# Grouped attention over a cache: K, P and q transposed as 32-bit words of two bf16, scores in 64-row tiles

## The chip, the cores and the metric

The kernel runs on one core of one Trainium2 chip. The metric is device time in microseconds from start to end of one execution; the figure compared is the median of several runs. It is written engine by engine: TensorE (PE), VectorE (DVE), ScalarE (ACT), GpSimd (POOL) and the sync engine (SP), which issues nearly all DMAs. Each engine works through its own list in order, and semaphores tie the lists together.

## What is computed

```python
B, Sq, D = 32, 4, 1024
Hq, Hkv, Sk, Dh = 32, 4, 2048, 128          # everything bf16
q = (x @ wq).reshape(B, Sq, Hq, Dh).transpose(0, 2, 1, 3)
k = jnp.repeat(k_cache, Hq // Hkv, axis=1)  # k_cache, v_cache: [B, Hkv, Sk, Dh]
v = jnp.repeat(v_cache, Hq // Hkv, axis=1)
scores = jnp.einsum("bhqd,bhkd->bhqk", q, k) * (Dh ** -0.5)
p = softmax(scores)
o = jnp.einsum("bhqk,bhkd->bhqd", p, v)
return o.transpose(0, 2, 1, 3).reshape(B, Sq, Hq * Dh) @ wo
```

A batch has 32 query rows for each of the four K/V heads (8 query heads times 4 tokens): the 128 rows of its score matrix are 4 heads times 32. K and V are 2 MB each per batch, and 32 batches of both are 134 MB of the 151 MB that are read.

## The kernel before

**Loads.** SP issues x, four slices of wq (each holds two of the eight slices `kt` of the contraction), K of batches 0 to 2, and then, batch by batch, K of batch b + 3 and V of batch b. There are three buffers each: K of batch b waits until the last K fill of batch b - 3 is done (line 149), V of batch b until the PV product of batch b - 3 is (line 158). Four slices of wo go between, over the memory of wq. The last V comes in four pieces, one for each head (line 161).

**q.** x is transposed (line 185) and q is projected with weight slices as the stationary operand (line 192): 8 slices times 32 heads, 128 x 128 each, so that q comes out with the head dimension on the partitions. Eight copies on DVE and ACT (lines 203 and 205) bring it to `QT_sb`.

**One batch.** K arrives with sequence rows on the partitions and has to be turned so that the head dimension is on them. `pe_fill` (line 223) does that with 64 bf16 transposes of 128 x 128, eight to a PSUM bank, in `NFILL` = 8 fills; `evac` copies each fill to `KT_sb`, fills 2, 3, 5 and 7 on DVE (line 233) and the others on ACT (line 235). The banks come from a ring of four (`slot`), and whoever takes a bank waits for the copy that empties it. `pe_qk` makes the scores: four column tiles of 32 (one per head) times four chunks of 512 sequence positions; the weights of a tile are loaded with the first chunk (line 260), and the other three use them again (`_matmul_held`, line 16). Then follow the maximum on DVE (line 300), exp on ACT with a running sum (line 305), 16 bf16 transposes of P (`pe_pt`, line 241) with two copies on DVE (line 247), 64 matmuls of P with V (`pe_pv`, line 268), the division by the sum on ACT (line 285), and one transpose of the result (line 291). Every eight batches the output projection runs (line 316).

**The order.** PE's list for step i: scores of batch i, the transpose of result i - 3, the fills of batch i + 1, PV of batch i - 2, the transposes of P of batch i. On ACT exp of batch i stands between the copies of fills 1 and 4, on DVE the maximum stands ahead of all copies of the step. Ahead of step 0 come x, q and the fills of batch 0. After the last step come PV of batch 30, the last PV head by head (line 380), and the last output projection with it.

Of the kernel before, what the change touches and what calls it, by code (L numbers as in the profile page):

```python
# [5 lines left out]
ACT = mybir.ActivationFunctionType  # L6
# [6 lines left out]
def _matmul_held(nc, eng, out, lhsT, rhs, tile_position, start, stop):  # L13


    return eng.add_instruction(mybir.InstMatmult(  # L16
        name=nc.get_next_instruction_name(),
        engine=eng.engine,
        start_tensor_calc=start,
        stop_tensor_calc=stop,  # L20
        tile_size=(128, 32),
        tile_position=tile_position,
        ldweights=False,
        ins=[eng.lower_ap(rhs), eng.lower_ap(lhsT, for_matmul_weights=True)],
        outs=[eng.lower_ap(out)],
    ))
# [46 lines left out]
def bass_standalone__gqa_block_cached__sampling_kernel(  # L73
# [12 lines left out]
    NT = B * Sq  # L86
# [5 lines left out]
    TV = T // C  # L92
    KT = D // 128
    NKB = 3
    NVB = 3
    NFILL = 8
    TB = T // NFILL
# [10 lines left out]
    with ExitStack() as es:  # L108
# [7 lines left out]
        KT_sb = sbuf("KT_sb", [128, TV, G, R * C], BF16)  # L116
        QT_sb = sbuf("QT_sb", [128, B, Hq, Sq], BF16)
        oT_sb = sbuf("oT_sb", [128, Hq, NT], BF16)
        P_sb = sbuf("P_sb", [128, Sk], BF16)
        PT_sb = sbuf("PT_sb", [128, 2, TV, 128], BF16)  # L120
# [3 lines left out]
        y_sb = sbuf("y_sb", [128, NOG, NC], BF16)  # L124
        ident = sbuf("ident", [128, 128], BF16)
        mx = sbuf("mx", [128, B], F32)
        negmx = sbuf("negmx", [128, B], F32)
        ssum = sbuf("ssum", [128, B], F32)
        rinv = sbuf("rinv", [128, B], F32)
# [5 lines left out]
        def ps_q(h):  # L135
            t = ps_s if h < 16 else ps_r[:, :, :].rearrange("p a b -> p (a b)")
            return t[:, (h % 16) * 128:(h % 16 + 1) * 128]
# [32 lines left out]
        for b in range(B):  # L170
# [10 lines left out]
            pattern=[[-1, 128]], channel_multiplier=1), ["ident0"], "ident")  # L181

# [6 lines left out]
        p.op("dve", lambda e: e.tensor_copy(xT_sb.rearrange("p a b -> p (a b)"), ring[2].bitcast(BF16)), ["xT"], "xT_evac")  # L189
        for kt in range(KT):  # L190
            for h in range(Hq):
                p.op("pe", lambda e, kt=kt, h=h: e.matmul(  # L192
                    ps_q(h), lhsT=w_sb[:, kt, h * Dh:(h + 1) * Dh], rhs=xT_sb[:, kt, :],
                    start=(kt == 0 and h % 4 == 0), stop=(kt == KT - 1), skip_group_check=True),
                    ["xT_evac", ("wq", kt // 2)],
                    ("qproj" if h == Hq - 1 else ("q", h // 4)) if kt == KT - 1 and h % 4 == 3 else None)
        for j in (4, 5, 6, 7, 0, 1, 2, 3):
            src = (ps_s if j < 4 else ps_r[:, :, :].rearrange("p a b -> p (a b)"))[:, (j % 4) * 512:(j % 4 + 1) * 512]
            src = src.rearrange("p (hh b s) -> p hh b s", hh=4, b=B, s=Sq)
            dst = QT_sb[:, :, 4 * j:4 * j + 4, :].rearrange("p b hh s -> p hh b s")  # L200
            w = "qproj" if j == Hq // 4 - 1 else ("q", j)
            if j % 2 == 0:
                p.op("dve", lambda e, s=src, d=dst: e.tensor_copy(d, s), [w], ("qe", j))  # L203
            else:
                p.op("act", lambda e, s=src, d=dst: e.activation(d, s, ACT.Copy), [w], ("qe", j))  # L205


        freed = [("qe", 4 + n) for n in range(NRING)]
# [8 lines left out]
        def pe_fill(b, f):  # L217
            buf, waits = slot(("kt", b, f))
            buf = slot_of["kt", b, f] = buf.bitcast(BF16)
            for q in range(TB):  # L220
                c, v = q // (TB // C), q % (TB // C)
                t = c * TV + f * TB // C + v
                p.op("pe", lambda e, q=q, t=t: e.transpose(  # L223
                    buf[:, q * 128:(q + 1) * 128], K_sb[:, b % NKB, t, :], ident[:, :]),
                    waits + [("k", b), "ident"] if q == 0 else [], ("fill", b, f) if q == TB - 1 else None)

        def evac(b, f):
            buf = slot_of["kt", b, f]
            waits = [("fill", b, f)] + ([("qk", b - 1)] if b else [])
            dst = KT_sb[:, f * TB // C:(f + 1) * TB // C, :, :].rearrange("p v g (r c) -> p (v g) r c", c=C)  # L230
            src = buf.rearrange("p (c m r) -> p m r c", c=C, r=R)
            if f in DVE_FILLS:
                p.op("dve", lambda e: e.tensor_copy(dst, src), waits, ("kt", b, f))  # L233
            else:
                p.op("act", lambda e: e.activation(dst, src, ACT.Copy), waits, ("kt", b, f))  # L235

        def pe_pt(i, f, ready):
            buf, waits = slot(("pt", i, f))
            buf = slot_of["pt", i, f] = buf.bitcast(BF16)
            for q in range(8):  # L240
                p.op("pe", lambda e, q=q: e.transpose(  # L241
                    buf[:, q * 128:(q + 1) * 128], P_sb[:, (8 * f + q) * 128:(8 * f + q + 1) * 128], ident[:, :]),
                    waits + [ready] if q == 0 else [], ("ptf", i, f) if q == 7 else None)

        def evac_pt(i, f):
            buf = slot_of["pt", i, f]
            p.op("dve", lambda e: e.tensor_copy(PT_sb[:, i % 2, 8 * f:8 * f + 8, :].rearrange("p t q -> p (t q)"), buf),  # L247
                 [("ptf", i, f)] + ([("pv", i - 2)] if i > 1 else []), ("pt", i, f))


        def pe_qk(i):
            waits = [("kt", i, f) for f in range(NFILL)]
            waits += [("qe", j) for j in range(Hq // 4)] if i == 0 else [("exp", i - 1)]
            for c in range(4):
                for g in range(G):
                    out = ps_s[32 * g:32 * (g + 1), c * 512:(c + 1) * 512]
                    lhsT = QT_sb[:, i, REP * g:REP * (g + 1), :]
                    rhs = KT_sb[:, 4 * c:4 * (c + 1), g, :]
                    if c == 0:
                        mm = lambda e, a=(out, lhsT, rhs), g=g: e.matmul(  # L260
                            a[0], lhsT=a[1], rhs=a[2], start=True, stop=True, tile_position=(0, 32 * g))
                    else:
                        mm = lambda e, a=(out, lhsT, rhs), g=g: _matmul_held(
                            nc, e, *a, tile_position=(0, 32 * g), start=True, stop=True)
                    p.op("pe", mm, waits, ("qk", i) if (c, g) == (3, G - 1) else None)

        def pv_mm(buf, i, g, t, waits, done):
            p.op("pe", lambda e: e.matmul(  # L268
                buf[32 * g:32 * (g + 1), 0:Dh],
                lhsT=PT_sb[:, i % 2, t, 32 * g:32 * (g + 1)],  # L270
                rhs=V_sb[:, i % NVB, g, t, :],
                start=(t == 0), stop=(t == TV - 1), tile_position=(0, 32 * g)), waits, done)
# [10 lines left out]
        def o_evac(i):  # L283
            buf = slot_of["o", i]
            p.op("act", lambda e: e.activation(o_sb[:, :], buf[:, 0:Dh], ACT.Copy, scale=rinv[:, i:i + 1]),  # L285
                 [("pv", i), ("rinv", i)] + ([("oT", i - 1)] if i else []), ("o", i))
# [6 lines left out]
        def ot_evac(i):  # L293
            buf = slot_of["ot", i]
            p.op("act", lambda e: e.activation(  # L295
                oT_sb[:, :, i * Sq:(i + 1) * Sq], buf[:, 0:128].rearrange("p (h s) -> p h s", s=Sq), ACT.Copy),
                [("oT", i)], ("ot", i))

        def softmax_max(i):
            p.op("dve", lambda e: e.tensor_reduce(mx[:, i:i + 1], ps_s[:, :], AX.X, ALU.max), [("qk", i)], ("mx", i))  # L300
            p.op("dve", lambda e: e.tensor_scalar(negmx[:, i:i + 1], mx[:, i:i + 1], -scale, None, op0=ALU.mult),  # L301
                 [("mx", i)], ("negmx", i))

        def softmax_exp(i):
            p.op("act", lambda e: e.activation(  # L305
                P_sb[:, :], ps_s[:, :], ACT.Exp, bias=negmx[:, i:i + 1], scale=scale, accum_out=ssum[:, i:i + 1]),
                [("negmx", i)] + ([("ptf", i - 1, 1)] if i else ["qproj"]), ("exp", i))

        def softmax_rinv(i):
            p.op("dve", lambda e: e.reciprocal(rinv[:, i:i + 1], ssum[:, i:i + 1]), [("exp", i)], ("rinv", i))  # L310


        def oproj_mm(buf, n, heads, waits, done):
            for h in heads:
                for j in range(4):
                    p.op("pe", lambda e, h=h, j=j: e.matmul(  # L316
                        buf[32 * j:32 * (j + 1), 0:NC],
                        lhsT=oT_sb[:, h, 32 * n:32 * (n + 1)],
# [22 lines left out]
        for i in range(B):  # L341
# [20 lines left out]
            if i == L:  # L362
                p.op("dve", lambda e: e.tensor_scalar(P_sb[:, :], P_sb[:, :], rinv[:, L:L + 1], None, op0=ALU.mult),  # L363
# [13 lines left out]
        def pv_last(g):  # L377
            buf, waits = slot(None)
            for t in range(TV):
                p.op("pe", lambda e, t=t: e.matmul(  # L380
                    buf[:, 0:32], lhsT=V_sb[:, L % NVB, g, t, :], rhs=PT_sb[:, L % 2, t, 32 * g:32 * (g + 1)],
# [4 lines left out]
                oT_sb[:, 8 * g:8 * (g + 1), L * Sq:(L + 1) * Sq], buf[:, 0:32].rearrange("p (h s) -> p h s", s=Sq)),  # L386
# [73 lines left out]
```

## Time and profile before

| | |
|---|---|
| median of 6 runs | 383.03 us (382.2 to 384.02) |
| profiled execution | 382.05 us |
| its span | 380.3 us |
| PE, DVE, ACT busy | 277.0, 274.8, 207.4 us (73%, 72%, 55%) |
| PE weight loads busy | 217.6 us (57%) |
| PE instructions | 5927 matmuls and transposes, 5543 weight loads |
| moved by DMA | 152.3 MB, 401 GB/s over the span |

The profile is of one execution. Busy time of an engine is the time in which at least one of its instructions ran; durations in a group are means of one instruction, and PE's overlap each other, so that the distance between two is shorter than the duration of one. The chain that ended last is followed back from the last instruction, at each step to what released it. "L223" is line 223 of the kernel. q1 is the queue of the program's own transfers, q8 that of its instructions.

### The profile page before, as it was taken

To read this page: it belongs to the slowest core of one execution; us is meant where nothing else is said; L and a number is where in the kernel's file an instruction comes from. 1 tells how busy PE (TensorE), PEld (TensorE's weight loads), DVE (VectorE), ACT (ScalarE), POOL (GpSimd) and SP (SyncE) were. 2 spreads that over 40 slices of the span, in tenths; PEclk is the share of its full clock that TensorE was granted. 3 is DMA by queue.
4 is the path that set the end of the run, shared out by engine and by line. 5 is a ranking of instruction groups with operands and counts; after the bars stand their busy time and mean duration, and the time that the engine had idled before them with its cause. 6 is when DMAs were issued, how large, how long until landed. Compare 5 with 4: busy or idle time off the path is not lost.

```text
span 380.3 us, 12207 instructions
## 1 busy us (share of the span) xinstructions
PE 277.0 (73%) x5927; PEld 217.6 (57%) x5543; DVE 274.8 (72%) x302; ACT 207.4 (55%) x259; POOL 0.7 (0%) x6
## 2 busy tenths in 40 slices
PE   2876878883837677788777777878777678877756
PEld 1874656662726555566555556656555456655545
DVE  0006999995538395699988884989888776998741
ACT  1005777771615461677666664677666446766630
POOL 0000000000000000000000000000000000000000
PEclk9998999999768699999999999999999999999989
DMA  8999999999999999999999999999999999999981
GB/s 331 427 429 431 413 410 418 411 394 410 402 411 410 423 414 417 411 416 415 418 415 418 415 417 418 415 419 416 416 415 415 415 416 424 415 417 408 370 320 44
DMA packets 27250, 152.30 MB, mean 401 GB/s; under 512 B 1472, under 2 KB 1984, under 8 KB 22592
## 3 DMA queue, kind: packets, MB, share of 16 engines
q1 hardware_dynamic: 27104, 151.49, 97.5%
q8 instruction: 45, 0.74, 0.8%
q10 hardware_dynamic: 96, 0.03, 0.0%
q14 instruction: 5, 0.04, 0.0%
HBM read 151.26 MB, written 0.26 MB: 398 GB/s over the span
## 4 chain that ended last, share of the span: by engine, by line
DMA 56%; PE 17%; ACT 13%; DVE 10%; issue 2%; SPq 1%
DMA K_sb<-in_k_cache_dram 56%; ACT KT_sb L235 7%; ACT P_sb L305 6%; DVE KT_sb L233 5%; PE ps_r L223 4%; DVE mx L300 4%; PE ps_r L316 3%; PE ps_r L268 3%; PE ps_r L241 3%; PE ps_s L16 2%; PE ps_s L316 1%; PE ps_s L260 1%; DVE PT_sb L247 1%; PE ps_r L380 0%; SPq L145 0%
## 5 line engine op out<-in xcount | busy, mean ns | idle before, releaser
L223 PE MATMUL ps_r<-ident,K_sb 128*128 128x128 bf16 x2048 | 139.9, 226 | 59.3 <-DMA K_sb<-in_k_cache_dram 34.8
L233 DVE COPY KT_sb<-ps_r 128x1024 bf16<-128x1024 bf16 x128 | 147.9, 1217 | 31.1 <-PE ps_r L223 30.9
L223 PEld LDWEIGHTS ps_r<-ident,K_sb 128*128 128x128 bf16 x2048 | 122.3, 101 | 78.2 <-DMA K_sb<-in_k_cache_dram 35.6
L235 ACT ACTIVATE KT_sb<-ps_r 128x1024 bf16<-128x1024 bf16 x128 | 124.3, 1026 | 70.3 <-PE ps_r L223 70.3
L300 DVE TENSOR_REDUCE mx<-ps_s 128x1 f32<-128x2048 f32 x32 | 73.3, 2292 | 6.1 <-PE ps_s L16 2.1
L305 ACT ACTIVATE P_sb<-ps_s,negmx 128x2048 bf16<-128x2048 f32 x32 | 63.1, 1970 | 2.1 <-DVE negmx L301 2.1
L247 DVE COPY PT_sb<-ps_r 128x1024 bf16<-128x1024 bf16 x64 | 41.3, 686 | 18.6 <-PE ps_r L241 17.0
L268 PE MATMUL ps_r<-V_sb,PT_sb 128*32 128x128 bf16 x1984 | 34.2, 222 | 18.4 <-ACT KT_sb L235 13.5
L268 PEld LDWEIGHTS ps_r<-V_sb,PT_sb 128*32 128x32 bf16 x1984 | 28.7, 98 | 23.7 <-ACT KT_sb L235 21.3
L295 ACT ACTIVATE oT_sb<-ps_r 128x128 bf16<-128x128 bf16 x31 | 8.6, 278 | 54.1 <-PE ps_r L291 54.1
L241 PE MATMUL ps_r<-ident,P_sb 128*128 128x128 bf16 x512 | 35.0, 223 | 3.0 <-DVE P_sb L363 2.5
L241 PEld LDWEIGHTS ps_r<-ident,P_sb 128*128 128x128 bf16 x512 | 29.4, 99 | 6.6 <-DVE P_sb L363 2.7
L16 PE MATMUL ps_s<-KT_sb,QT_sb 128*32 128x512 bf16 x384 | 27.0, 387 | 0.0
L291 PEld LDWEIGHTS ps_r<-ident,o_sb 128*128 128x128 bf16 x31 | 3.0, 98 | 26.1 <-issue 26.1
L203 DVE CAST QT_sb<-ps_r 128x512 bf16<-128x512 f32 x2 | 1.3, 686 | 22.4 <-PE ps_r L192 22.4
L285 ACT ACTIVATE o_sb<-ps_r,rinv 128x128 bf16<-128x128 f32 x31 | 11.4, 367 | 11.1 <-PE ps_r L268 11.1
L316 PE MATMUL ps_r<-w_sb,oT_sb 128*32 128x256 bf16 x384 | 11.8, 273 | 5.3 <-issue 4.1
L205 ACT ACTIVATE QT_sb<-ps_r 128x512 bf16<-128x512 f32 x2 | 1.1, 594 | 25.9 <-PE ps_r L192 25.9
L260 PE MATMUL ps_s<-KT_sb,QT_sb 128*32 128x512 bf16 x128 | 13.0, 396 | 2.5 <-DVE KT_sb L233 1.7
L192 PE MATMUL ps_s<-P_sb,w_sb 128*128 128x128 bf16 x128 | 9.3, 231 | 7.5 <-DMA w_sb<-in_wq_dram 7.5
L316 PEld LDWEIGHTS ps_r<-w_sb,oT_sb 128*32 128x32 bf16 x384 | 10.1, 97 | 6.5 <-issue 5.4
L192 PEld LDWEIGHTS ps_s<-P_sb,w_sb 128*128 128x128 bf16 x128 | 8.1, 104 | 8.0 <-issue 4.3
(27 smaller groups left out, 65.8 us busy)
## 6 DMA issues: line engine op xcount, KB each, us to landing
K_sb<-in_k_cache_dram SPq DMA_DIRECT2D x32, 2048.0 KB, 25.2
V_sb<-in_v_cache_dram SPq DMA_DIRECT2D x31, 2048.0 KB, 27.0
w_sb<-in_wq_dram SPq DMA_DIRECT2D x4, 2048.0 KB, 14.6
w_sb<-in_wo_dram SPq DMA_DIRECT2D x4, 2048.0 KB, 24.1
V_sb<-in_v_cache_dram SPq DMA_DIRECT2D x4, 512.0 KB, 11.4
P_sb<-in_x_dram SPq DMA_DIRECT2D x1, 256.0 KB, 2.7
out_dram<-y_sb SPq DMA_DIRECT2D x14, 16.0 KB, 9.4
out_dram<-y_sb ACTq DMA_DIRECT2D x2, 16.0 KB, 1.8
```

Of the source, the lines that this page charges most:

```text
L16: return eng.add_instruction(mybir.InstMatmult(name=nc.get_next_instruction_name(), engine=eng.engine, start_tensor_calc=start, stop_tenso ...
L192: p.op("pe", lambda e, kt=kt, h=h: e.matmul(ps_q(h), lhsT=w_sb[:, kt, h * Dh:(h + 1) * Dh], rhs=xT_sb[:, kt, :], start=(kt == 0 and h % 4 ...
L223: p.op("pe", lambda e, q=q, t=t: e.transpose(buf[:, q * 128:(q + 1) * 128], K_sb[:, b % NKB, t, :], ident[:, :]), waits + [("k", b), "iden ...
L233: p.op("dve", lambda e: e.tensor_copy(dst, src), waits, ("kt", b, f))
L235: p.op("act", lambda e: e.activation(dst, src, ACT.Copy), waits, ("kt", b, f))
L241: p.op("pe", lambda e, q=q: e.transpose(buf[:, q * 128:(q + 1) * 128], P_sb[:, (8 * f + q) * 128:(8 * f + q + 1) * 128], ident[:, :]), wai ...
L247: p.op("dve", lambda e: e.tensor_copy(PT_sb[:, i % 2, 8 * f:8 * f + 8, :].rearrange("p t q -> p (t q)"), buf), [("ptf", i, f)] + ([("pv", ...
L260: mm = lambda e, a=(out, lhsT, rhs), g=g: e.matmul(a[0], lhsT=a[1], rhs=a[2], start=True, stop=True, tile_position=(0, 32 * g))
L268: p.op("pe", lambda e: e.matmul(buf[32 * g:32 * (g + 1), 0:Dh], lhsT=PT_sb[:, i % 2, t, 32 * g:32 * (g + 1)], rhs=V_sb[:, i % NVB, g, t, : ...
L300: p.op("dve", lambda e: e.tensor_reduce(mx[:, i:i + 1], ps_s[:, :], AX.X, ALU.max), [("qk", i)], ("mx", i))
L305: p.op("act", lambda e: e.activation(P_sb[:, :], ps_s[:, :], ACT.Exp, bias=negmx[:, i:i + 1], scale=scale, accum_out=ssum[:, i:i + 1]), [( ...
L316: p.op("pe", lambda e, h=h, j=j: e.matmul(buf[32 * j:32 * (j + 1), 0:NC], lhsT=oT_sb[:, h, 32 * n:32 * (n + 1)], rhs=wo_sb[:, h, NC * j:NC ...
```

## The change

Two neighbouring bf16 values are taken as one 32-bit word and transposed as such, with a float identity. A 128 x 128 transpose of words moves two sequence rows of K (or two columns of P, or two halves of heads of q) at once. What comes out has, on partition r, word r of each row pair.

- K: a fill is four transposes of words in place of eight of bf16. Word r < 64 of a pair of rows holds elements 2r and 2r + 1 of the first row's head dimension, word r >= 64 those of the second row. So `KT_sb` has even and odd elements interleaved, the first rows of the pairs on partitions 0 to 63 and the second rows on 64 to 127. Each transpose writes every fourth word of a bank, and the copy is of 512 contiguous words.
- Scores: 64-row tiles. The lower half of the partitions makes the scores of the even rows, the upper half those of the odd rows, into different banks. The even and the odd elements of the head dimension (`w`) are two matmuls that add up. That is 32 matmuls of 512 columns in place of 16, and 16 weight loads in place of 4: `half` 0 loads the weights, `half` 1 uses them again. `TT` is 8, `DW` 64.
- Exp reads the two halves of the banks in turn, so that P comes out in the order of the sequence. P is transposed in 8 words' transposes instead of 16, its copies are of 512 words, and PV reads its weights in steps of two elements.
- q: x is now the stationary operand and wq the moving one (64 matmuls of 512 columns, weights loaded once per `kt`), which puts tokens on the partitions; eight copies bring q to `q_sb` (in the memory of `KT_sb`), 33 transposes of words turn it, and nine copies bring it to `QT_sb` (33 head slots, since the upper half needs each head shifted by one).
- To make room, the output and half of the transposed result lie over parts of `QT_sb` that are used up, and the per-batch statistics have four columns.

```diff
-def _matmul_held(nc, eng, out, lhsT, rhs, tile_position, start, stop):
+def _matmul_held(nc, eng, out, lhsT, rhs, tile_size, tile_position, start, stop):
...
-    NFILL = 8
-    TB = T // NFILL
+    NFILL = TT
...
-        KT_sb = sbuf("KT_sb", [128, TV, G, R * C], BF16)
-        QT_sb = sbuf("QT_sb", [128, B, Hq, Sq], BF16)
+        KT_sb = sbuf("KT_sb", [128, TT, G, R * C, 2], BF16)
+        q_sb = KT_sb[:, :, :, :, :].rearrange("p a g n w -> p (a g n w)")[:, 0:(Hq + 2) * Dh]
+        QT_sb = sbuf("QT_sb", [128, B, Hq + 1, Sq, 2], BF16)
...
+        p.op("pool", lambda e: e.tensor_copy(identf[:], ident[:]), ["ident"], "identf")
+        for h in (0, Hq + 1):
+            p.op("pool", lambda e, h=h: e.memset(q_sb[:, h, :], 0.0), [], ("qpad", h))
...
         for kt in range(KT):
-            for h in range(Hq):
-                p.op("pe", lambda e, kt=kt, h=h: e.matmul(
-                    ps_q(h), lhsT=w_sb[:, kt, h * Dh:(h + 1) * Dh], rhs=xT_sb[:, kt, :],
...
+            for j in QJ:
+                out, lhsT, rhs = ps_q(j), xT_sb[:, kt, :], w_sb[:, kt, 512 * j:512 * (j + 1)]
+...
+        NQ = (Hq + 1 + 3) // 4
+        for m in range(NQ):
+            slots = range(4 * m, min(4 * m + 4, Hq + 1))
+            buf = ps_q(m % 4)
+            for n, c in enumerate(slots):
...
+                waits += ([("qe", m - 4)] if m >= 4 else [("qs", m)]) if n == 0 else []
+                p.op("pe", lambda e, n=n, c=c, buf=buf: e.transpose(
+                    buf[:, 128 * n:128 * (n + 1)], words(q_sb[:, c:c + 2, :].rearrange("p h d -> p (h d)")), identf[:, :]),
+                    waits, ("qt", m) if c == slots[-1] else None)
+...
         def pe_fill(b, f):
-            for q in range(TB):
...
-                p.op("pe", lambda e, q=q, t=t: e.transpose(
-                    buf[:, q * 128:(q + 1) * 128], K_sb[:, b % NKB, t, :], ident[:, :]),
+            for c in range(C):
+                t = 2 * (c * TT + f)
+                p.op("pe", lambda e, c=c, t=t: e.transpose(
+                    buf.rearrange("p (n c) -> p n c", c=C)[:, :, c],
+                    words(K_sb[:, b % NKB, t:t + 2, :].rearrange("p t d -> p (t d)")), identf[:, :]),
...
         def evac(b, f):
-            dst = KT_sb[:, f * TB // C:(f + 1) * TB // C, :, :].rearrange("p v g (r c) -> p (v g) r c", c=C)
-            src = buf.rearrange("p (c m r) -> p m r c", c=C, r=R)
+            dst = words(KT_sb[:, f, :, :, :].rearrange("p g n w -> p (g n w)"))
...
         def pe_pt(i, f, ready):
-            for q in range(8):
+            for q in range(4):
                 p.op("pe", lambda e, q=q: e.transpose(
-                    buf[:, q * 128:(q + 1) * 128], P_sb[:, (8 * f + q) * 128:(8 * f + q + 1) * 128], ident[:, :]),
+                    buf[:, q * 128:(q + 1) * 128], words(P_sb[:, (4 * f + q) * 256:(4 * f + q + 1) * 256]), identf[:, :]),
...
         def pe_qk(i):
-            for c in range(4):
-                for g in range(G):
-                    out = ps_s[32 * g:32 * (g + 1), c * 512:(c + 1) * 512]
-                    lhsT = QT_sb[:, i, REP * g:REP * (g + 1), :]
-                    rhs = KT_sb[:, 4 * c:4 * (c + 1), g, :]
...
+            for w in range(2):
+                for half in range(2):
+                    for g in range(G):
+                        for par in range(2):
+                            rows = slice(DW * par, DW * (par + 1))
+                            out = ps_s[32 * g:32 * (g + 1), (2 * par + half) * 512:(2 * par + half + 1) * 512]
+                            lhsT = QT_sb[rows, i, REP * g + 1 - par:REP * (g + 1) + 1 - par, :, w]
+                            rhs = KT_sb[rows, 4 * half:4 * half + 4, g, :, w]
+...
         def softmax_exp(i):
             p.op("act", lambda e: e.activation(
-                P_sb[:, :], ps_s[:, :], ACT.Exp, bias=negmx[:, i:i + 1], scale=scale, accum_out=ssum[:, i:i + 1]),
+                P_sb[:, :].rearrange("p (n a) -> p n a", a=2), ps_s[:, :].rearrange("p (a n) -> p n a", a=2), ACT.Exp, ...),
```

## The prediction

> **What bounds the kernel now.** I read the page's busy slices and its table of DMA queues first, then the chain that ended last, then the groups by line, and last the timelines of the first 42 and last 50 us.
>
> ```profile
> PEclk9998999999768699999999999999999999999989
> DMA  8999999999999999999999999999999999999981
> GB/s 331 427 429 431 413 410 418 411 394 410 402 411 410 423 414 417 411 416 415 418 415 418 415 417 418 415 419 416 416 415 415 415 416 424 415 417 408 370 320 44
> q1 hardware_dynamic: 27104, 151.49, 97.5%
> q8 instruction: 45, 0.74, 0.8%
> ```
>
> The DMA line is at 9 in every slice from the second to the last but one: K and V stream at about 415 GB/s and no engine makes them wait. PE and DVE at 73% and 72% are not the bound. Work removed from PE, DVE or ACT between 40 and 350 us buys nothing by itself.
>
> The q8 line matters more than its 0.8%. Its bytes are TensorE's program: 0.74 MB over 5927 + 5543 PE instructions is 64.5 bytes each. Each of the 45 fetches is 16 KB and lands on one of the 16 DMA engines, whose share of the current load then comes late. The trace's landing records (16 per load, one per engine) show it: K0's shares land from 27.7 to 29.4 us, K20's from 233.9 to 240.2, K31's from 343.7 to 351.8. The first share moves 9.98 us per batch ((343.7 - 233.9) / 11), the last 10.15. The 16 delays at K31 add up to 65.9 us after 40 fetches, 1.65 us per fetch, on 8 engines in turn (eight shares are 7.6 us late, six not at all). A load counts as landed with its last share, so the kernel runs at the pace of the engines that carry the fetches.
>
> ```profile
> 329.12 22.70 DMA K_sb<-in_k_cache_dram
> ...
> 358.29 1.08 PE ps_r L268 x64
> 359.37 1.00 PE ps_r L241 x16
> 360.37 0.33 PE ps_s L260 x4
> 360.70 0.67 PE ps_s L16 x12
> ...
> 361.39 2.30 DVE mx L300
> ...
> 363.90 2.07 ACT P_sb L305 x2
> ...
> 367.00 1.89 PE ps_r L241 x16
> 368.89 0.11 PE ps_r L291
> 368.99 1.61 PE ps_r L268 x43
> ```
>
> This is the end of the chain, from K31's landing at 351.81. The PV product of batch 28 at 358.29 has an ACT copy ahead of it in the chain, but V28's last share lands at 358.15, so DMA released it. PE works in order: P's transposes (L241), scores 31 (L260, L16), the maximum, exp, P again, PV 30 and the output projection follow it. The end is V28's landing plus 22 us of chain. V31's four pieces (last shares 369.4, 370.8, 372.0, 373.3) land about 1 to 2 us ahead of their use (371.3 to 374.6).
>
> ```profile
> L223 PE MATMUL ps_r<-ident,K_sb 128*128 128x128 bf16 x2048 | 139.9, 226 | 59.3 <-DMA K_sb<-in_k_cache_dram 34.8
> L233 DVE COPY KT_sb<-ps_r 128x1024 bf16<-128x1024 bf16 x128 | 147.9, 1217 | 31.1 <-PE ps_r L223 30.9
> L235 ACT ACTIVATE KT_sb<-ps_r 128x1024 bf16<-128x1024 bf16 x128 | 124.3, 1026 | 70.3 <-PE ps_r L223 70.3
> L247 DVE COPY PT_sb<-ps_r 128x1024 bf16<-128x1024 bf16 x64 | 41.3, 686 | 18.6 <-PE ps_r L241 17.0
> L203 DVE CAST QT_sb<-ps_r 128x512 bf16<-128x512 f32 x2 | 1.3, 686 | 22.4 <-PE ps_r L192 22.4
> L205 ACT ACTIVATE QT_sb<-ps_r 128x512 bf16<-128x512 f32 x2 | 1.1, 594 | 25.9 <-PE ps_r L192 25.9
> ```
>
> **K's copies (hidden).** A fill still takes one bank, now of 512 words. The nearest rows for 512 four-byte elements are L203 (686 ns) and L205 (594), against 1217 and 1026. A batch saves 4 x 0.53 us on DVE and 4 x 0.43 on ACT. Per batch DVE then has 2.29 + 0.3 + 6 x 0.69 = 6.7 us and ACT 5.2, under the 10.15 us of DMA: worth nothing outside start and end. P's copies keep 0.69.
>
> **The 32-bit transpose, X (unknown).** A batch has 32 + 8 instead of 64 + 16. A bf16 one takes 0.056 us (8 in 0.45 us of weight loads). No row has a 4-byte transpose, so the bounds are 0.056, as if the size of a word didn't matter, and 0.224, if both operands cost by their bytes and the two costs multiply. I take 0.112, twice the time for twice the bytes; PE time for transposes is then unchanged. The rest of PE's batch (PV 1.08, scores 1.0, others 0.3) makes 7.0 us with it, 11.5 at the upper bound. DMA's 10.15 is passed at X = 0.19.
>
> The Trainium skill speaks on both sides here. "PSUM — Partial Sum Buffer", Specifications, says that any non-contiguous pattern slows matmuls significantly, and K's new transposes write every fourth word; "TensorE: Matmul & The Clock Gate", Weight-path perf modes, leaves 4-byte weights out of the fast weight load. The same page, Terms, says that a transpose mode makes FP32 four times faster. No row of this trace shows any of the three; the first two would put the sum at the upper rival below, the third at the forecast.
>
> **Start of the kernel.** Now the last weight chunk is done at 28.3 us, q is copied by 30.1, K0's fills run from 29.5 to 34.1, and SP, waiting for the last fill, issues K3 at 34.45. K2's shares land from 37.5 on; a load's first bytes come about 2 us after its issue (x: 0.74 to 3.4; V31's first piece: 359.4 to 362.6 with 1.25 us of transfer). DMA therefore runs dry only if K3 is issued after about 35.6.
> In the changed kernel q is projected with 64 matmuls and 8 weight loads in place of 512 instructions. The fetch at 17.0 us came after 272 PE instructions; only 154 now lie ahead of K0's fills, so the weights land at 23.2 (the other shares) and not 24.5. The last two slices take 16 x 0.216 = 3.5 us (0.65 us for 12 score matmuls in fours is 0.216 each), ending at 26.8; eight copies end near 27.9. Added: 33 transposes and nine copies (0.69 and 0.59) through four banks, each group waiting for the copy four back. At 0.112 that is 27.4 to 31.0, and the eight fills end at 34.5: K3 goes out as before, cost nothing. POOL's float identity and two zeroed pads, which the new transposes wait for, follow its 1.5 us of work at the start and are over long before 27. The formula for larger X is 27.5 + 65 X; it passes 35.6 at X = 0.125, and each further 0.01 costs 0.65 us that nothing covers, since the stream never has slack again.
>
> **Instructions fetched.** Matmuls go from 5927 to 5000 (K -1024, P -256, scores +512, q -192 +33), weight loads from 5543 to 4432 (K -1024, P -256, scores 128 to 512, q -248 +33). The 2038 fewer at 64.5 bytes are 131 KB, 8 fetches of 16 KB, one per affected engine. Ahead of V28's end there were 41 (eight engines five times, one six); now 33 to 34, the worst engine five. One fetch less on it is 1.5 us (K31's 7.6 us over five). V28 to V31 land 1.5 us earlier, and the chain with them: -1.5.
>
> **The end of the chain.** P's transposes of batch 30: 16 in 1.00 us, now 8 x 0.112: -0.1. Those of batch 31 run at half clock (PEclk 0.50 from 367 to 370 us): 1.89, now 8 x 0.224 = 1.8, -0.1; if only bf16 slows, -0.9, most of which V30's landing (366.7 after the shift) takes back. Scores 31: 32 matmuls in 64-row tiles. If eight overlap, as four column tiles do now, the stream stays at four times 0.216; eight more loads ahead at 0.025 (four in 0.10) add 0.2 at most, I take +0.1. If the row halves don't overlap, +0.9. Exp reads two halves of PSUM in turn; L235 reads with steps at (1026 - 594)/512 = 0.84 ns per element, L205's pace, so I take 0; the bound is twice the exp, about +1.7 on the chain, hidden elsewhere. The maximum, L363 and PV keep their times (PV's weights are now read in steps of two, but a load takes 0.014 us there, 64 in 0.90, under its matmuls; bound +0.9 if doubled). Sum: -1.5 - 0.1 - 0.1 + 0.1 = -1.6.
>
> The profiled execution took 382.05 us (span 380.3); with -1.6 that is 380.4 (378.7). It lies 1.0 under the median of 383.03, so the forecast for the median is 381.4.
>
> **Rivals.**
> *The 32-bit transpose is slow (ends slower).* One mechanism on PE, at the start and in every batch. It loses from X = 0.16, where 0.65 per 0.01 above 0.125 has eaten the gain: 384 at 0.17, 385.5 at 0.19. Beyond, PE binds: at 0.224, K3 at 42, then 31 batches of 11.5 and some 21 us of tail after 43: near 421. For it: nothing in the trace shows a 4-byte operand in a transpose, and the output is strided. Against it: half as many instructions.
> *Fetches don't fall* because a 4-byte transpose takes several instructions. Then only the -0.1 of the chain is left: 382.9, no change.
> *Row halves or exp are slower at the end.* The shorter chain stays and 0.8 or 1.7 goes back: 382.2 or 383.1.
>
> **Numbers.** Forecast 0.52 (its own range 379.9 to 382.2: from -3.1, with two fetches less on the worst engine or a faster P, to -0.8); slow transpose 0.26, of which 0.15 lies above 385.5; no fewer fetches 0.10; slower end 0.12. A change under 0.2%, 0.77 us, can't be told from none. Faster: the forecast and 0.07 of the slower end, 0.59; same: 0.15; slower: 0.26. The range 379.9 to 385.5 leaves out the 0.15 and a little below.
>
> **What would show it.** Right: q8 near 37 packets; K31's or V28's last share 1 to 2 us earlier; DMA at 9 through the start; K3 issued by 35.6; 32-bit transposes about 0.11 us apart; copies of K near 0.69 and 0.59. Wrong: a DMA slice under 9 near 40 us, PE above 95% busy with DMA below 9, q8 at 45 or more, or scores of 2 us ahead of the last maximum.

## The result, and the profile after

The changed kernel takes 381.43 us (median of 25 runs) against 382.94 (50 runs of before beside it): ratio 0.9963, 95% interval 0.9954 to 0.9972. A second measurement beside other runs gave 381.59 against 382.78, 0.9971 (0.9958 to 0.9983). That is 1.2 to 1.5 us faster; 381.4 was forecast. One execution of each of two runs below (empty instructions, and copies at the durations of before) took 1405 us, where the others took 381 to 383; it is left out of the figures.

The page of the changed kernel has these slices and queues (digits are busy tenths of a slice; the queue rows give packets, MB, share of 16 engines):

```profile
PEclk9999999987668598999999899999999999999969
DMA  8999999999999999999999999999999999999970
q1 hardware_dynamic: 27104, 151.49, 97.3%
q8 instruction: 37, 0.61, 0.7%
```

The same 27104 packets of data keep DMA at 9 from the second slice to the last but two, as before. What differs is q8: 37 fetches of instructions in place of 45, as counted in advance. The end of the chain (start in us, duration, what; "..." marks lines left out):

```profile
328.49 28.48 DMA V_sb<-in_v_cache_dram
...
357.11 1.08 PE ps_r L320 x64
358.19 1.02 PE ps_r L285 x8
359.21 0.35 PE ps_s L311 x8
...
360.28 2.30 DVE mx L352
...
362.79 2.07 ACT P_sb L357 x2
...
365.89 1.97 PE ps_r L285 x8
...
367.97 1.86 PE ps_r L320 x64
...
376.33 0.42 DVE QT_sb L381
```

The PV product of batch 28 (PV 28, L320) now starts at 357.11 and is put down to the transfer of V of batch 28 (V28), whose last share lands at 357.0, 1.2 us earlier than before. V31's pieces land 0.9 to 1.0 earlier (the last at 372.3). Of the 1.18 us gained at PV 28, 0.77 are left at the last copy of the output (376.33 against 377.10 before). The groups by line (x count, then busy us, mean ns) and the start of the kernel from the timeline:

```profile
L267 PEld LDWEIGHTS ps_r<-identf,K_sb 128*128 128x128 f32 x1024 | 121.8, 150 | 59.6 <-DMA K_sb<-in_k_cache_dram 50.2
L277 DVE COPY KT_sb<-ps_r 128x512 f32<-128x512 f32 x128 | 85.0, 688 | 52.6 <-PE ps_r L267 51.4
L279 ACT COPY KT_sb<-ps_r 128x512 f32<-128x512 f32 x128 | 69.8, 593 | 84.5 <-PE ps_r L267 84.4
```

```profile
27.49 3.58 PEld L240 LDWEIGHTS ps_s<-identf,KT_sb 128*128 128x128 f32 x33 [2.54 <-issue]
31.04 3.52 PEld L267 LDWEIGHTS ps_r<-identf,K_sb 128*128 128x128 f32 x32
34.84 0.33 SPq L163 DMA_DIRECT2D K_sb<-in_k_cache_dram  x1
...
39.96 0.42 PEld L267 LDWEIGHTS ps_r<-identf,K_sb 128*128 128x128 f32 x4 [0.65 <-DVE KT_sb L277]
```

The copies of K take 0.69 and 0.59 us, a 32-bit transpose 3.58 / 33 = 0.108 us (q, contiguous output) and 0.42 / 4 = 0.105 to 3.52 / 32 = 0.110 (K, every fourth word; four in one go at 39.96, 32 from 31.04). K of batch 3 (K3) goes out at 34.84. The profiled execution of the changed kernel is a late one of its runs (382.8 us): the two output transfers on ACT's queue took 2.15 us to issue, against 0.96 before. A fetch of instructions ran beside that issue, from 377.4 on, but one did so in the kernel before too (from 377.2), so the cause of the delay isn't shown. In the second measurement's profile they took 1.08, and the span is 379.6.

### The profile page after: what moved, and what is told of

It is laid out like the page before. It is cut to its first block, busy times and chain, and to the rows that moved or that the text cites. A ratio compares the mean times of both kernels' runs of the same rounds, so it can differ in the third digit from the quotient of the medians.

```text
span 380.7 us, 10182 instructions
## 1 busy us (share of the span) xinstructions
PE 276.5 (73%) x5000; PEld 210.5 (55%) x4432; DVE 215.4 (57%) x307; ACT 156.0 (41%) x263; POOL 1.3 (0%) x9
## 3 DMA queue, kind: packets, MB, share of 16 engines
q1 hardware_dynamic: 27104, 151.49, 97.3%
## 4 chain that ended last, share of the span: by engine, by line
DMA 63%; PE 21%; ACT 7%; DVE 6%; issue 1%; SPq 0%
DMA V_sb<-in_v_cache_dram 44%; DMA K_sb<-in_k_cache_dram 14%; DMA w_sb<-in_wq_dram 5%; ACT P_sb L357 5%; DVE mx L352 4%; PE ps_r L285 4%; PE ps_r L320 4%; PE ps_r L368 3%; PE ps_r L267 3%; ACT KT_sb L279 2%; PE ps_s L311 2%; PE ps_s L16 2%; PE ps_s L368 1%; PE ps_s L240 1%; DVE KT_sb L226 0%
## 5 line engine op out<-in xcount | busy, mean ns | idle before, releaser
L267 PE MATMUL ps_r<-identf,K_sb 128*128 128x128 f32 x1024 | 132.6, 290 | 50.6 <-DMA K_sb<-in_k_cache_dram 47.5
L267 PEld LDWEIGHTS ps_r<-identf,K_sb 128*128 128x128 f32 x1024 | 121.8, 150 | 59.6 <-DMA K_sb<-in_k_cache_dram 50.2
L277 DVE COPY KT_sb<-ps_r 128x512 f32<-128x512 f32 x128 | 85.0, 688 | 52.6 <-PE ps_r L267 51.4
L279 ACT COPY KT_sb<-ps_r 128x512 f32<-128x512 f32 x128 | 69.8, 593 | 84.5 <-PE ps_r L267 84.4
L292 DVE COPY PT_sb<-ps_r 128x512 f32<-128x512 f32 x64 | 41.3, 687 | 58.9 <-PE ps_r L285 58.9
L357 ACT ACTIVATE P_sb<-ps_s,negmx 128x2048 bf16<-128x2048 f32 x32 | 63.3, 1977 | 9.3 <-DVE negmx L353 9.2
L320 PE MATMUL ps_r<-V_sb,PT_sb 128*32 128x128 bf16 x1984 | 35.3, 226 | 31.2 <-DMA V_sb<-in_v_cache_dram 24.9
L320 PEld LDWEIGHTS ps_r<-V_sb,PT_sb 128*32 128x32 bf16 x1984 | 29.9, 100 | 37.9 <-ACT KT_sb L279 31.7
L285 PE MATMUL ps_r<-identf,P_sb 128*128 128x128 f32 x256 | 36.3, 287 | 3.6 <-DVE P_sb L415 2.2
L285 PEld LDWEIGHTS ps_r<-identf,P_sb 128*128 128x128 f32 x256 | 28.6, 145 | 7.4 <-DVE P_sb L415 2.3
L311 PE MATMUL ps_s<-KT_sb,QT_sb 64*32 64x512 bf16 x512 | 26.5, 390 | 0.9 <-DVE KT_sb L277 0.9
L16 PE MATMUL ps_s<-KT_sb,QT_sb 64*32 64x512 bf16 x512 | 26.1, 383 | 0.0
L311 PEld LDWEIGHTS ps_s<-KT_sb,QT_sb 64*32 64x32 bf16 x512 | 7.3, 90 | 10.4 <-issue 5.2
L16 PE MATMUL ps_s<-w_sb,P_sb 128*128 128x512 bf16 x32 | 9.1, 411 | 0.0
```

The source lines that it names most:

```text
L16: return eng.add_instruction(mybir.InstMatmult(name=nc.get_next_instruction_name(), engine=eng.engine, start_tensor_calc=start, stop_tenso ...
L267: p.op("pe", lambda e, c=c, t=t: e.transpose(buf.rearrange("p (n c) -> p n c", c=C)[:, :, c], words(K_sb[:, b % NKB, t:t + 2, :].rearrange ...
L277: p.op("dve", lambda e: e.tensor_copy(dst, buf), waits, ("kt", b, f))
L279: p.op("act", lambda e: e.copy(dst, buf), waits, ("kt", b, f))
L285: p.op("pe", lambda e, q=q: e.transpose(buf[:, q * 128:(q + 1) * 128], words(P_sb[:, (4 * f + q) * 256:(4 * f + q + 1) * 256]), identf[:, :]),
L292: p.op("dve", lambda e: e.tensor_copy(dst, buf), [("ptf", i, f)] + ([("pv", i - 2)] if i > 1 else []), ("pt", i, f))
```

## The experiments

The theory: the gain is the eight fetches that no longer delay a share of the loads. The rival: it is the shorter copies, or the transposes. All ratios are to the kernel before on the same chip. The column V28 is the landing of its last share in the trace's landing records, 358.2 us in the kernel before and 357.0 in the changed one. "Loop" is the distance between the PV products of two batches while nothing waits for DMA: 8.63 us before, 8.28 after.

| kernel | q8 | loop, us | V28, us | ratio (95%) |
|---|---|---|---|---|
| changed, again | 37 | 8.27 | 356.9 | 0.9971 (0.9958 to 0.9983) |
| changed, much slower copies | 37 | 9.42 | 356.8 | 1.0019 (1.0008 to 1.0030) |
| changed, copies as before | 37 | 8.71 | 356.9 | 0.9968 (0.9952 to 0.9984) |
| before, PV in pairs to batch 27 | 38 | 9.55 | 357.2 | 0.9994 (0.9981 to 1.0007) |
| before, PV in pairs to batch 23 | 39 | 9.55, then 8.63 | 357.5 | 0.9963 (0.9948 to 0.9978) |
| changed, PV in pairs | 30 | 9.13 | 355.7 | 0.9941 (0.9920 to 0.9962) |
| the same again | 30 | 9.13 | 355.6 | 0.9954 (0.9936 to 0.9972) |
| changed, PV steps split | 45 | 8.41 | 358.4 | 1.0050 (1.0028 to 1.0071) |
| changed, P as bf16 | 39 | 8.25 | 357.2 | 0.9972 (0.9961 to 0.9984) |

**The changed kernel, again.** 

> The changed kernel itself, beside the other three. 381.2 to 381.7, ratio to before 0.995 to 0.997, q8 37.

It came out so; it is the reference on that chip for three of the runs below.

**The copies made slow again, too slow.**

```diff
+            if b >= 1:
+                dst = KT_sb[:, f, :, :, :].rearrange("p g n w -> p w (g n)")
+                src = buf.bitcast(BF16).rearrange("p (n w) -> p w n", w=2)
```

> The changed kernel with K's copies of batches 1 to 31 made over the same words as bf16 in steps of two, which should take the times of before (1.2 us on DVE, 1.0 on ACT in place of 0.69 and 0.59). No PE instruction changes. Theory: q8 stays at 37, the copies are hidden under 10 us of DMA per batch, 381.3 to 381.8, ratio 0.996 to 0.997. Rival (shorter copies are the gain): back to 382.6 or more, ratio 0.999 or more.

The rival's number came, 1.0019. But DMA did what the theory says: q8 37, V28 at 356.8, the last piece of V31 at 372.2. The chain shows what was late:

```profile
340.43 1.08 PE ps_r L326 x64
...
349.85 1.08 PE ps_r L326 x64
...
359.27 1.08 PE ps_r L326 x64
```

PV 28 starts 2.4 us after V28 landed, 9.42 us after PV 27. ACT's strided copies took 1.33 us, longer than in the kernel before (1.03), and the loop runs through them and exp in turn. The third output projection holds PE for 4 to 5 us from about 310 us on; a loop of 9.42 wins back some 0.6 us per 10 us of DMA, and only four steps lead from there to PV 28. So the run showed a limit that the prediction did not have, and did not test the copies of before.

**The copies at the durations of before.** As above, with contiguous bf16 on ACT.

> The changed kernel with K's copies of batches 1 to 31 at the durations of before: 1.2 us on DVE (bf16 in steps of two), 1.0 on ACT (1024 contiguous bf16). PE's list as in the changed kernel. In the run with still slower copies the step from one PV product to the next took 9.42 us, too slow to recover from the third output projection; here about 8.6, as in the kernel before. Theory: q8 37, PV 28 released by V28's landing at 357.0, 381.3 to 381.9, ratio 0.9955 to 0.9975. Rival (copies are the gain): 382.6 or more, ratio 0.999 or more.

```profile
L281 DVE COPY KT_sb<-ps_r 128x1024 bf16<-128x1024 bf16 (+1 forms) x128 | 154.4, 1281 | 31.1 <-PE ps_r L267 31.0
L285 ACT ACTIVATE KT_sb<-ps_r 128x1024 bf16<-128x1024 bf16 x124 | 120.4, 1025 | 66.8 <-PE ps_r L267 66.8
```

DVE is busy for 67 us more than in the changed kernel and ACT for 52 us more, and the time is the changed kernel's (0.9968 beside 0.9971). The rival, which asked for 0.999 or more, falls. Against what was expected, PV 28 did not wait for V28 here:

```profile
352.02 0.67 PE ps_r L267 x4
...
356.60 0.92 ACT KT_sb L285
357.57 1.08 PE ps_r L328 x64
```

The chain runs from K31's landing through ACT's copies to PV 28, 0.6 us after V28's landing at 356.9. So once V28 comes earlier, the old copies are the next limit. In the profiles the shorter ones are worth about 0.5 us there (PV 28 at 357.57 against 357.00 in the changed kernel again); the medians, 381.8 and 381.6 with intervals of 0.5 to 0.6 us to either side, can't resolve it.

**The fetches alone, in the kernel before.** The PV product of two heads goes through one 64-column weight load and 256 moving columns, half of which is thrown away: more work, fewer instructions.

```diff
+            W = 2
             for t in range(TV):
...
+                for h in range(G // W):
+                    p.op("pe", lambda e, t=t, h=h: e.matmul(
+                        buf[32 * W * h:32 * W * (h + 1), 0:W * Dh],
+                        lhsT=PT_sb[:, i % 2, t, 32 * W * h:32 * W * (h + 1)],
+                        rhs=V_sb[:, i % NVB, W * h:W * (h + 1), t, :],
...
```

> The kernel before, its transposes and scores untouched, with the PV product of batches 0 to 27 made in pairs of heads: 64 weight columns and 256 moving columns, of which half is used, so 64 PE instructions in place of 128 per batch, and four copies of 32 rows on ACT in place of one. 1792 fewer PE instructions are 7 fetches. Theory: q8 at 38, V28's last share about 1.3 us earlier than 358.2, time 381.4 to 381.9, ratio 0.996 to 0.998, although PE works 0.6 us and ACT 0.9 us longer per batch. Rival (fetches don't matter; the gain of the change is its copies or transposes): 382.9 to 383.3, ratio 1.000 or above.

V28 came 0.9 us earlier and the time didn't follow (0.9994): the loop is 9.55 us (PV 1.94 in place of 1.08, and three more copies on ACT), and PV 28 starts at 358.99, late by itself as in the run with slow copies. The same with pairs for batches 0 to 23 only:

> The kernel before with the PV product in pairs of heads for batches 0 to 23 only, so that the loop is as short as before (8.6 us in place of 9.55) after the third output projection. 1536 fewer PE instructions are 6 fetches. Theory: q8 39, PV 28 released by V28's landing at 357.3, 0.8 to 1.3 us below the kernel before, ratio 0.9965 to 0.998. Rival (fetches don't matter): ratio 0.9995 to 1.001.

```profile
q8 instruction: 39, 0.64, 0.7%
```

```profile
352.09 0.63 PE ps_r L223 x8
...
356.63 0.92 ACT KT_sb L235
357.60 1.08 PE ps_r L268 x64
```

0.9963. With bf16 transposes, the old copies and more PE work (295.4 us busy against 277.0), six fetches less give as much as the whole change, as far as the intervals can tell. PV 28 starts at 357.60, 0.7 us earlier than before; V28's landing at 357.5 and the end of the last copy from K31's landing at 357.55 fall together there.

**Fewer still, in the changed kernel.** The same pairs, batches 0 to 27.

> The changed kernel with the PV product of batches 0 to 27 in pairs of heads in the same way. Theory: q8 at 30, a further 1.2 to 1.5 us, 379.9 to 380.3, ratio 0.992 to 0.9935. Rival: 381.4 or above, ratio 0.996 or above.

> The changed kernel with PV in pairs of heads for batches 0 to 27 once more, for a narrower interval: q8 30, its loop of 9.13 us has recovered from the third output projection when V28 lands near 355.7. Theory: 379.9 to 380.6, ratio to before 0.992 to 0.9945, clearly under the changed kernel's 0.997. Rival (fetches don't matter): 0.996 or above.

380.19 and 380.22 us in two measurements, each 2.4 us under the kernel before on its chip, where the changed kernel was 1.2 to 1.5 under: the fastest version here. Both ratios lie just above the range expected for them (up to 0.9935 and 0.9945), and the second interval reaches the changed kernel's 0.9971. The loop is 9.13 us and has recovered when V28 lands (second measurement):

```profile
327.93 27.69 DMA V_sb<-in_v_cache_dram
...
355.75 1.08 PE ps_r L323 x64
```

**As many as before, in the changed kernel.** Eleven of sixteen PV steps in two halves, batches 0 to 23.

```diff
+                    if i < 24 and 0 < t <= 11:
+                        for d in range(2):
+                            p.op("pe", lambda e, g=g, t=t, d=d: e.matmul(
+                                buf[32 * g:32 * (g + 1), 64 * d:64 * (d + 1)], ...
```

> The changed kernel with eleven of the sixteen PV steps of batches 0 to 23 each made in two halves of 64 columns: the same products, 88 more PE instructions per batch, 2112 in all, and some 0.7 us more PE time in each of these batches, none in the last eight. Theory (fetches): q8 at 45, V28's last share near 358.2 as in the kernel before, the batch loop below 9.2 us and so recovered before the end, time 1.0 to 1.5 us above the changed kernel, 382.4 to 382.9, ratio to before 0.9985 to 1.0005. Rival (shorter copies and transposes): they are untouched, 381.3 to 381.7, ratio 0.9955 to 0.997.

q8 is 45 and V28 is back at 358.4, but the time overshot: 384.99. Its executions fall in two groups, three at 382.8 to 383.0 (near the predicted loss; the profiled one is among them) and nine from 384.5 to 386.8. The chain of the profiled one has 7.2% "issue", against 1% in the changed kernel, and PE's timeline shows where (time in brackets: idle before):

```profile
294.42 0.41 PE L311 MATMUL ps_s<-KT_sb,QT_sb 64*32 64x512 bf16 x5
297.16 0.41 PE L311 MATMUL ps_s<-KT_sb,QT_sb 64*32 64x512 bf16 x3 [2.33 <-issue]
```

PE stops in the middle of the scores, with nothing to wait for, while a fetch of q8 runs from 294.7 to 295.8, and goes on 1.4 us after it. The same stands at 145.05 (3.61 us, fetch 146.1 to 147.2) and 180.6 (3.44 us, fetch 181.5 to 182.6). After the first 35 us the trace has nine such stops of over 1.6 us, and each ends 1.2 to 1.5 us after a fetch does. The kernel before has two, with the same distance, the longer one in an output projection beside a fetch from 150.2 to 151.3; the changed kernel has none:

```profile
147.78 2.35 PE L316 MATMUL ps_r<-w_sb,oT_sb 128*32 128x256 bf16 x77
152.70 0.40 PE L316 MATMUL ps_r<-w_sb,oT_sb 128*32 128x256 bf16 x7 [2.58 <-issue]
```

So PE was out of instructions, as far as a trace can show it. That this is also what makes the nine executions later is argued from the one profile, not shown: those nine have none. The stops cost the profiled one something too: its PV 28 starts at 358.98, 0.6 us after V28.

**P as bf16 again.**

> The changed kernel with one part undone: P is transposed as bf16 again (16 transposes with weights read in steps of two, copies of 1024 bf16). 512 more PE instructions are 2 fetches on 2 of the 8 affected engines, the transposes of a batch take 1.0 us either way, the copies 0.69. Theory: q8 39, V28 0 to 1.4 us later according to whether the engine that lands last has one more; time 381.5 to 382.6, ratio 0.997 to 0.9995. Rival (the words' transposes of P are the gain on the chain at the end): 0.9 us or more from the cold transposes of batch 31 alone, whatever V28 does.

0.9972, the changed kernel's time, with V28 unmoved and V31's last piece at 373.5 in the profiled execution. The part that transposes P as words is worth nothing that can be measured.

**Empty instructions.**

```diff
+            if 1 <= i < 29:
+                for _ in range(73):
+                    p.op("pe", lambda e: e.nop(nofuse=True))
```

> The changed kernel with 73 empty instructions added to TensorE's list after the scores of each of batches 1 to 28 (2044 in all, about as many as the change removed); the work is the same. Theory (the gain is the eight instruction fetches that no longer delay a share of the loads): q8 back to 45 packets, V28's last share about 1.2 us later than in the changed kernel, time 1.0 to 1.6 us above it, at 382.5 to 383.0, ratio to before 0.999 to 1.001. Rival (the gain is shorter copies and transposes): TensorE has 3 us of slack per batch, so 381.4 as the changed kernel, ratio 0.996. If the empty instructions themselves fill TensorE's slack, the DMA row falls below 9 and the run tells nothing.

q8 stayed at 37: the empty instructions did not arrive as fetched ones, so the run says nothing on the theory. It measured 0.9978 (0.9966 to 0.9991). Its profile is of the execution of 1405 us, so only the packet count is taken from it.

## Why the prediction was right, point by point

- *What bounds it.* Right: DMA, at the pace of the engines that carry the fetches. At K31 the delays against the five earliest shares add up to 55.7 us after 32 fetches (1.74 each; 1.65 before). Over the runs of the table V28 moves in step with the number of fetches, whatever else was changed: 30 fetches 355.6 and 355.7, 37 356.8 to 357.0, 38 357.2, 39 357.2 and 357.5, 45 358.2 and 358.4. That V28 released PV 28 in the kernel before, and not the ACT copy ahead of it in the chain, was read rightly: in the run with the copies as before, where such a copy released it, it started 5.55 us after K31's landing; here that would be 357.4, and it started at 358.29.
- *Fetches.* 37 as counted. The page "Runtime: NRT & Kernel Launch" of the Trainium skill, Instruction fetch mechanics, says that instructions are refilled in blocks of 16 KiB and that crossing a block is mostly hidden. The blocks agree (0.61 MB in 37 packets); hidden they were not, neither for V28 nor in the stops of the split kernel. The step on V28 was 1.2 us, not 1.5: its last share had five fetches ahead of it in place of six, as forecast, but came 1.36 us less behind the first share (7.98 against 9.34), and the first share came 0.2 later. K31 came no earlier (352.0 against 351.8): a fetch at 349.8 still fell ahead of its last share, so that engine had five in both kernels. Which load gains thus hangs on where the fetches fall.
- *The 32-bit transpose.* 0.105 to 0.110 against 0.112 taken. The stride over every fourth word costs nothing that shows (0.105 to 0.110 with it, 0.108 without). "PSUM — Partial Sum Buffer", Specifications, of the Trainium skill says that a pattern with gaps slows matmuls significantly; for these transposes it does not, and the measurement decides.
- *The start.* Weights at 23.3 us, fills from 31.04, K3 at 34.84 (forecast 23.2, 31.0, 34.5; the prediction's own formula gives 34.8 at its 0.112); K3's first share landed at 42.4 (42.3 before), so DMA never ran dry.
- *Copies hidden.* Right up to the end of the chain, shown by the run with the old durations; there they are worth the 0.5 us of its profile, which the sum had at nothing. The reason given, engine time under 10.15 us per batch, was not enough: the loop through PE, DVE and ACT must also be short enough to win back the output projection before the end. 8.28, 8.63 and 9.13 were; 9.42 and 9.55 were not. (The parts named for PE's batch add up to 6.9 and 11.3 us, not 7.0 and 11.5; nothing hangs on it.)
- *The end of the chain.* Mis-sized in small terms: P's transposes +0.02 and +0.08 (-0.1 each forecast), scores +0.05 (+0.1), exp 0 (1977 against 1970 ns), and PV 30 +0.25 (1.86 against 1.61; none forecast). With 1.18 gained at PV 28 that leaves the 0.77 of the two profiles, where 1.6 was forecast. PV 30 fell wholly into a stretch at half the TensorE clock: the trace has it granted from 363.9 to 370.7, and from 366.8 to 370.2 before. What made the stretch longer isn't shown; the run with the old copies has 6.8 us of it too, with PE busier (5.81 us from 360 to 370, against 5.61 here and 5.78 before), the run with pairs to batch 23 has 3.4.
- *The number.* The medians moved by 1.2 to 1.5 us, more than the 0.8 of the profiles. The profiled execution of the kernel before, 382.05 us, lies 0.7 to 0.9 under its medians, those of the changed kernel lie above theirs (382.80 against 381.43, 381.68 against 381.59), and no trace shows what makes the other executions of before later. The forecast added that distance, 1.0, to the changed kernel as well. So the direction and the cause are as forecast, but that 381.4 was met so closely is luck: a gain taken too large and a distance that did not carry over offset each other.

## What to carry to other kernels

When every data queue is full, count the instructions: each 16 KB of a program is a transfer on the same engines, and a load is as late as its latest share. Fewer, larger TensorE instructions paid here even where they did useless work. Then ask whether the rest of the loop can still make up its interruptions before the end, since a saving on a hidden engine is worth little (here at most the 0.5 us at the end of the chain) and a loss on it shows only past that point.

## What was not expected

- A 2 us to 4 us stop of TensorE inside a burst, it seems for want of instructions, beside a fetch (2.33 us at 294.8, 3.61 at 145.05 in the kernel with 88 more instructions per batch; 2.58 at 150.1 in the kernel before).
- The fetches go to eight of the sixteen engines: at K31 in the kernel before, after 40 of them, eight shares are 7.6 to 7.9 us late, six less than 0.4, two 1.6 and 2.1.
- A 32-bit transpose costs the PE time of two bf16 ones, 0.105 to 0.110 us, with or without a strided output. The forecast took this value, but had no row for it.
